# A fused attention and expert kernel: float32 score products for the third query group, half of the first group's scaling on ScalarE, and another order of the first loads

## The chip, the cores and the metric

The kernel runs on one core of one Trainium2 chip. The metric is the device time of one execution in microseconds, the median of the runs shown. A profiled execution has a time of its own, and next to it a span, from its first to its last instruction.

## What is computed

Windowed attention with a few sink keys feeds a dense two-layer block, and that feeds a router with eight experts:

```python
scores = q @ k.T / sqrt(64);  keep = (key < 4) | (0 <= query - key < 128)   # 2 batches, 8 heads, 768 tokens
a = softmax(where(keep, scores, -1e9));  x = heads_to_rows(a @ v)           # 1536 x 512
h = x @ w_in;  x = max(0.01 * h, h) @ w_out                                 # 512 -> 2048 -> 512
active = x @ w_skip > 0;  e = argmax(x @ w_gate);  g = softmax(x @ w_gate)[e]
out = x + active * g * (relu(x @ w1[e]) @ w2[e])                            # eight experts, 512 -> 1024 -> 512
```

All inputs are float32 (`w_in` and `w_out` come as 64-bit words that are decoded to float32 on the chip).

## The kernel before

The 1536 tokens are six **groups** of 256, numbered g = 0 to 5; so the "third group" is g = 2. Each group goes through attention (`attention`), then through 16 **chunks** f = 0 to 15 of the dense block (`chunk`): line 802 is a chunk's first product (12 matmuls of 256 columns into a tile `h`), line 823 its second (6 matmuls of 512 columns into `acc`, or into the tiles `S` and `PV` for g = 1). While group g's chunks run, group g+1's attention is to be done beside them. Only the chunks of g = 0 and g = 1 are interleaved with each other, since each decoded weight (`decode_w`, lines 704, 706, 708, 675 on VectorE and 668 on ScalarE) comes once and serves all groups. At the end come the experts (`plan_routed`).

Attention of a group has four head pairs p = 0 to 3 and, in each, two blocks of 128 queries qt = 0, 1. One (p, qt) is an **item** (`item`): scores for two heads, mask and row minimum on VectorE (552), exponential with row sum on ScalarE (555), the sum's reciprocal on VectorE (559, 560), scaling of the probabilities (567 on GpSimd, or 564 on ScalarE for g = 1), transposes (583, 605), the product with the values (622), and the copies that put the result where the dense block reads it (628 and 629, or 637, 638, 639 and then 668, 675).

There are two ways to be exact with float32 data:

- g = 0 and 1 (`self.whole`) form the scores as one float32 product (line 545). Queries are copied into a tile `qz` whose other 64 rows are zero, so one key tile serves both heads.
- g = 2 to 5 split queries and keys into a high and a low float32r half (`prep_split`, `queries`): the key tile is made twice, with two ScalarE copies (504) and two VectorE subtractions (506) for each p; the queries are transposed twice over (648), copied (650) and subtracted (651) for each item. Then the score is two products of one pass each (549). The sink keys have such halves too (`sink_keys`, 480 and 482); for g = 2 they are made early, from the first group's keys.

The order of the work on each engine is not written out by hand. `Plan.op` collects operations with an engine, a cost, tiles read and written, and a priority `pr`; `Plan.run` goes through them with those costs and, whenever an engine is free, takes the ready operation with the lowest `pr` whose tiles can be had. A tag such as `w`, `kT` or `T` has a fixed number of buffers, which are given out in the order in which the operations that first use them were written. So an operation can be ready and yet be passed over, because a tile written earlier in the code has not been taken. What comes out is one fixed list for each engine.

Loads of the first group are in `blocks`: keys on ScalarE's DMA queue, queries and values on SP's. `load_w` brings the dense weights (512 KB each) on SP's queue. `constants` builds masks on VectorE from two tiny loads, `lim`.

Of the kernel before, what the change touches and what calls it, by code (L numbers as in the profile page):

```python
# [39 lines left out]
def c_pool1(n):  # L40
    return 162 + 0.83 * n
# [184 lines left out]
class Arm:  # L226
# [4 lines left out]
    def __init__(self, tc, io, cst, scr, xg, window_attention):  # L231
        self.tc, self.nc, self.io, self.c, self.scr, self.xg = tc, tc.nc, io, cst, scr, xg
        self.fast = window_attention
        self.whole = (0, 1)
        self.B, self.H, self.S, self.D = io["q"].shape
# [69 lines left out]
    def attention(self, g):  # L305
# [23 lines left out]
    def blocks(self, g, b, qp):  # L329
# [5 lines left out]
        def ld(t, a, p0, p1):  # L335
# [3 lines left out]
            if t != "v":  # L339
                eng, dma = ("ACT", nc.scalar) if g == 0 and t == "k" else ("SP", nc.sync)  # L340
# [30 lines left out]
    def load(self, g, b, qp, p):  # L371
# [114 lines left out]
    def prep_split(self, g, qp, p):  # L486

        P, nc = self.p, self.nc
        pr = 16 * (g - 1) + 4 * p - 6.5
        rk, rv = self.rk, self.rv  # L490
# [17 lines left out]
        for h in range(2):  # L508
            P.op("POOL", c_pool1(32), lambda h=h: nc.gpsimd.tensor_scalar(
                out=kT[h].tile.rearrange("p (j c) -> p j c", c=144)[:, 0:2, 128:144], in0=self.kss[:, p, h:h + 1, :].bitcast(F32).to_broadcast([128, 2, 16]),  # L510
                scalar1=1.0, scalar2=1.0, op0=ALU.mult, op1=ALU.mult), r=[("kss", (p, h, i)) for i in range(2)], w=[(kT[h], "s")], pr=pr)

# [9 lines left out]
    def item(self, g, qp, p, qt, whole):  # L522
# [8 lines left out]
        if not whole:  # L531
            self.queries(g, p, qt, pr)
# [7 lines left out]
        for h in range(2):  # L540
            sp = P.buf(("S", "h", "h")[(4 * p + 2 * qt + h) % 3] if g == 0 else spare if g == 2 else "S", [128, 512])

            def score(sp=sp, h=h):
                if whole:
                    nc.tensor.matmul(out=sp.tile[:, 0:ncol], lhsT=self.qz.tile[:, p % 2, h, 128 * qt:128 * qt + 128], rhs=kT.tile[:, 0, c0:c0 + ncol], start=True, stop=True)
                    return
# [4 lines left out]
            P.op("PE", 4 * ncol / 2.4 if whole else 2 * c_mm(ncol), score, r=[(self.qz, (p % 2, h)), (self.qz, ("z", h)), kT] if whole else [*qT, kT[h]], w=[sp], pr=pr, hold=[A, nm, sm])  # L551
# [9 lines left out]
        for h in range(2):  # L561
            if g == 1:
# [713 lines left out]
def constants(nc, cp, pool, c, n_sink, window, E):  # L1276
# [5 lines left out]

    lim = T("lim", [128, 4], I32)
# [93 lines left out]
```

## Time and profile before

| | |
|---|---|
| median of 3 runs | 577.86 us (577.76 to 581.44) |
| profiled execution: its time | 577.76 us |
| profiled execution: its span | 576.0 us, so 1.76 us lie outside it |
| busy: TensorE 528.3, VectorE 412.3, ScalarE 345.3, GpSimd 172.8 us | 92%, 72%, 60%, 30% of the span |
| first scores | 10.87 us |
| first chunk of g = 2 goes on to its end from | 201.57 us |

A busy share is an average over parts with different limits: TensorE is idle or slow at the start, in one stretch near a third of the span, and at the end. Matmuls are pipelined, so that a busy TensorE is not one at its peak; what a matmul adds to a chain is read from the chain of waits, where an L802 of 12 matmuls takes 1.44 us.

### The profile page before, as it was taken

The numbers are of one execution on the slowest core, as the hardware profiler recorded it, in microseconds if no ns is written. First come the engines' busy times: TensorE is split into PE (matmuls) and PEld (weight loads), VectorE is DVE, ScalarE is ACT, GpSimd is POOL, SyncE is SP. The second block draws the span as 40 slices with busy tenths as digits, with TensorE's granted clock in tenths as the row PEclk, the third lists the DMA queues.
The fourth block names the chain that finished last, engine by engine and source line by source line (L and its number), as shares of the span: only waits on it lengthen the run. The fifth ranks groups of instructions, "written<-read, shape, count | busy, mean of one in ns | idle before, by whom it ended". The sixth has DMA issues, their size and how long they took to land.

```text
span 576.0 us, 10376 instructions
## 1 busy us (share of the span) xinstructions
PE 528.3 (92%) x3378; PEld 463.8 (81%) x3378; DVE 412.3 (72%) x1184; ACT 345.3 (60%) x892; POOL 172.8 (30%) x288
## 2 busy tenths in 40 slices
PE   3789999999999699999999999999999789999993
PEld 2668898878888588888899888999988678888772
DVE  3679999989678587668766786675746547767771
ACT  2669875554557466667656766555655356666760
POOL 3422201140143434333233333210221223443343
PEclk9989999999999699999999999999999889999997
DMA  6996543511112201222112230113465448888770
GB/s 148 281 317 235 193 141 119 146 50 52 56 44 60 53 21 37 49 53 73 40 36 51 47 83 15 25 48 137 138 194 171 161 156 286 265 273 287 250 261 21
DMA packets 81088, 72.99 MB, mean 127 GB/s; under 512 B 58579, under 2 KB 66771, under 8 KB 81024
## 3 DMA queue, kind: packets, MB, share of 16 engines
q1 hardware_dynamic: 77168, 70.67, 40.6%
q0 software_dynamic: 1600, 1.04, 0.6%
q10 hardware_dynamic: 2256, 0.53, 0.5%
q8 instruction: 29, 0.48, 0.4%
q14 instruction: 35, 0.29, 0.2%
HBM read 65.93 MB, written 10.51 MB: 133 GB/s over the span
## 4 chain that ended last, share of the span: by engine, by line
PE 64%; DVE 15%; ACT 7%; DMA 5%; POOL 4%; issue 4%; ACTq 0%; POOLq 0%; DVEq 0%
PE h L802 16%; PE acc L823 13%; PE acc L1043 5%; PE PV L622 4%; PE h L1027 3%; PE T L583 3%; DMA wm<-in_moe_w_dram 2%; POOL P L567 2%; PE S L1027 2%; PE S L549 2%; DVE C L638 2%; PE PV L1027 2%; PE T L897 2%; ACT P L555 2%; DVE P L552 2%
## 5 line engine op out<-in xcount | busy, mean ns | idle before, releaser
L802 PE MATMUL h<-x,w 128*128 128x256 f32 x1128 | 154.2, 286 | 3.0 <-DVE gl L816 1.8
L802 PEld LDWEIGHTS h<-x,w 128*128 128x128 f32 x1128 | 144.3, 190 | 8.1 <-DVE gl L816 3.2
L823 PE MATMUL acc<-w,gh 128*128 128x512 f32 x308 | 100.2, 406 | 0.0
L668 ACT ACTIVATE w<-wm 128x1024 fp32r<-128x1024 f32 x64 | 67.7, 1061 | 42.6 <-DMA wm<-in_moe_w_dram 26.6
L567 POOL TENSOR_SCALAR P<-P,s 128x272 f32<-128x272 f32 (+1 forms) x80 | 42.9, 550 | 114.7 <-DVE s L560 98.6
L675 DVE TENSOR_TENSOR w<-wm,w 128x1024 fp32r<-128x1024 f32 x48 | 60.2, 1262 | 17.3 <-ACT w L668 15.7
L675 POOL TENSOR_TENSOR w<-wm,w 128x1024 fp32r<-128x1024 f32 x16 | 38.8, 2427 | 93.3 <-ACT w L668 49.1
L555 ACT ACTIVATE P<-P,s 128x272 f32<-128x272 f32 (+1 forms) x96 | 50.0, 521 | 25.7 <-DVE s L552 25.2
L813 ACT ACTIVATE t<-h 128x256 f32<-128x256 f32 x94 | 35.8, 380 | 47.8 <-PE h L802 47.6
L823 PE MATMUL acc<-w,gl 128*128 128x512 f32 x156 | 61.3, 393 | 0.0
L823 PEld LDWEIGHTS acc<-w,gh 128*128 128x128 f32 x308 | 52.9, 189 | 7.2
L814 DVE TENSOR_TENSOR h<-h,t 128x256 f32<-128x256 f32 x94 | 40.2, 428 | 19.4 <-ACT t L813 18.6
L815 ACT ACTIVATE gh<-h 128x256 fp32r<-128x256 f32 x92 | 34.9, 379 | 19.1 <-DVE h L814 18.6
L816 DVE TENSOR_TENSOR gl<-h,gh 128x256 fp32r<-128x256 f32 x92 | 38.5, 418 | 10.9 <-ACT gh L815 9.9
L552 DVE CUSTOM_DVE_ANT_0 P<-S,mk 128x272 f32<-128x272 f32 (+1 forms) x70 | 28.9, 412 | 12.6 <-PE S L549 10.9
L823 PEld LDWEIGHTS acc<-w,gl 128*128 128x128 f32 x156 | 29.3, 188 | 6.8
L583 PE MATMUL T<-idt,P 128*128 128x128 f32 x152 | 27.7, 295 | 6.9 <-DVE kT L506 4.9
L583 PEld LDWEIGHTS T<-idt,P 128*128 128x128 f32 x152 | 22.7, 204 | 12.3 <-POOL P L567 4.5
L589 ACT ACTIVATE AT<-T 128x256 fp32r<-128x256 f32 x60 | 20.0, 383 | 13.5 <-PE T L583 12.7
L590 DVE TENSOR_TENSOR AT<-T,AT 128x256 fp32r<-128x256 f32 x60 | 23.4, 418 | 6.5 <-ACT AT L589 5.3
L638 DVE TENSOR_TENSOR C<-PV,C 64x256 f32<-64x256 f32 x48 | 20.3, 422 | 10.0 <-ACT C L637 6.5
L1043 PE MATMUL acc<-w,gT 128*128 128x512 f32 x96 | 24.5, 400 | 2.0 <-POOL w L675 1.6
(256 smaller groups left out, 1087.4 us busy)
## 6 DMA issues: line engine op xcount, KB each, us to landing
wm<-in_moe_w_dram SPq DMA_DIRECT2D x64, 512.0 KB, 4.7
w<-in_moe_w_in_dram SPq DMA_DIRECT2D x14, 512.0 KB, 5.7
w<-in_moe_w_out_dram SPq DMA_DIRECT2D x14, 512.0 KB, 6.8
rq<-in_q_dram SPq DMA_DIRECT2D x64, 64.0 KB, 2.1
out_dram<-x SPq DMA_DIRECT2D x12, 256.0 KB, 2.2
rk<-in_k_dram SPq DMA_DIRECT2D x24, 96.0 KB, 2.2
rv<-in_v_dram SPq DMA_DIRECT2D x24, 96.0 KB, 2.5
scr<-x SPq DMA_DIRECT2D x1, 2056.0 KB, 9.2
```

What stands on the lines that cost most here:

```text
L552: P.op("DVE", 66 + 1.07 * ncol, lambda sp=sp, h=h: nc.vector.tensor_tensor_reduce(out=A.tile[:, 0:ncol, h], in0=sp.tile[:, 0:ncol], in1=ma ...
L555: P.op("ACT", 280 + 0.83 * ncol, lambda h=h: nc.scalar.activation(out=A.tile[:, 0:ncol, h], in_=A.tile[:, 0:ncol, h], func=AF.Exp, scale=- ...
L567: P.op("POOL", 245 + 0.83 * ncol, lambda h=h: nc.gpsimd.tensor_scalar(out=A.tile[:, 0:ncol, h], in0=A.tile[:, 0:ncol, h], scalar1=sm.tile[ ...
L583: nc.tensor.transpose(tt.tile[:, 2 * j + h, :], A.tile[:, o:o + 128, h], c["idt"])
L668: nc.scalar.activation(out=at(0), in_=view(src.tile), func=AF.Copy)
L675: P.op(lo, {"DVE": c_dve(n), "POOL": c_pool2(n)}[lo], lambda: eng[lo].tensor_tensor(out=at(1), in0=view(src.tile), in1=at(0).bitcast(F32), ...
L802: nc.tensor.matmul(out=h.tile, lhsT=wi.tile[:, a, 128 * k:128 * k + 128], rhs=xT.tile[:, b, k, :], start=k == 0 and n == 0, stop=k == self ...
L814: P.op("DVE", c_dve(256), lambda: nc.vector.tensor_tensor(out=h.tile, in0=h.tile, in1=t.tile, op=ALU.max), r=[t], w=[h], pr=fast)
L816: P.op("DVE", c_dve(256), lambda: nc.vector.tensor_tensor(out=gl.tile, in0=h.tile, in1=gh.tile.bitcast(F32), op=ALU.subtract), r=[h, gh], ...
L823: nc.tensor.matmul(out=acc[i].tile, lhsT=a.tile[:, q], rhs=wo.tile[:, b, :], start=first and n == 0, stop=last and n == 2)
L1027: nc.tensor.matmul(out=hp[a].tile, lhsT=xt.tile[:, i, k, :], rhs=w1[k][j].tile[:, 512 * a:512 * a + 512], start=k == 0 and n == 0, stop=k ...
L1043: nc.tensor.matmul(out=yp.tile, lhsT=gt.tile[:, a, 2 * n + j, :], rhs=w2[n][b].tile[:, 512 * j:512 * j + 512], start=n == 0 and j == 0 and ...
```

## The change

There are three edits. `self.mixed = 2` gives g = 2 the float32 score products of the first two groups: `prep_mixed` makes one key tile and both blocks' queries for a head pair at once, and the queries are loaded once and not twice; the sink halves for g = 2 are not made any more. In `item`, the scaling of the second head of g = 0 goes from GpSimd to ScalarE. The third edit is in the first loads: `blocks` is called ahead of the zeroing of `qz`, the keys of p = 1 to 3 are issued on SP's queue, and a one-element exponential stands at the head of ScalarE's list.

```diff
@@ Arm.__init__
+        self.mixed = 2
@@ Arm.attention
         if whole:
+            self.blocks(g, b, qp)
             if g == 0:
                 self.qz = self.p.buf("w", [128, 2, 2, 256])
...
-            self.blocks(g, b, qp)
@@ blocks.ld
-                eng, dma = ("ACT", nc.scalar) if g == 0 and t == "k" else ("SP", nc.sync)
+                eng, dma = ("ACT", nc.scalar) if g == 0 and t == "k" and p0 == 0 else ("SP", nc.sync)
@@ load
-            two = 2 if t == "q" else 1
+            two = 2 if t == "q" and g != self.mixed else 1
@@ prep_split: its part on the keys is now prep_keys, without these lines
-        elif g - 1 in self.whole:
-            self.sink_keys(p, ("ks", p), lambda a: self.ks[a, p, :], pr)
@@ new
+    def prep_mixed(self, p, pr):
...
+        kT = self.kT = P.buf("kT", [128, 1, 432])
+        qT = self.qT = [P.buf("qT", [128, 256]) for _ in range(2)]
...
+        for h in range(2):
+            P.op("POOL", 100 + 0.9 * 256, lambda h=h: nc.gpsimd.memset(qT[h].tile[64 - 64 * h:128 - 64 * h, :], 0.0), w=[(qT[h], 0)], pr=pr - 1)
+        P.op("PE", 3 * C_TR, lambda: [nc.tensor.transpose(pk.tile[:, j, :], flat(rk, j), idt) for j in range(3)], r=[rk], w=[pk], pr=pr, hold=[kT])
...
+        P.op("ACT", c_act(384, True), lambda: nc.scalar.activation(out=col(0, 128), in_=pk.tile, func=AF.Copy), r=[pk], w=[(kT, 0)], pr=pr)
...
+        P.op("PE", 2 * C_TR, lambda: [nc.tensor.transpose(pq.tile[:, j, :], flat(rq, j), idt) for j in range(2)], r=[rq], w=[pq], pr=pr, hold=qT)
+        for h in range(2):
+            rows = slice(64 * h, 64 * h + 64)
+            P.op("ACT", c_act(256, True), lambda rows=rows, h=h: nc.scalar.activation(
+                out=qT[h].tile[rows, :], in_=pq.tile[rows].rearrange("p j c -> p (j c)"), func=AF.Copy, scale=-0.125), r=[pq], w=[(qT[h], 1)], pr=pr)
@@ prep_split
+        if g == self.mixed:
+            self.prep_mixed(p, pr)
+        else:
+            self.prep_keys(g, qp, p, pr)
@@ item
-        if not whole:
+        native = whole or g == self.mixed
+        if not native:
             self.queries(g, p, qt, pr)
...
-                if whole:
-                    nc.tensor.matmul(out=sp.tile[:, 0:ncol], lhsT=self.qz.tile[:, p % 2, h, 128 * qt:128 * qt + 128], rhs=kT.tile[:, 0, c0:c0 + ncol], start=True, stop=True)
+                if native:
+                    l = self.qz.tile[:, p % 2, h, 128 * qt:128 * qt + 128] if whole else qT[h].tile[:, 128 * qt:128 * qt + 128]
+                    nc.tensor.matmul(out=sp.tile[:, 0:ncol], lhsT=l, rhs=kT.tile[:, 0, c0:c0 + ncol], start=True, stop=True)
...
-            if g == 1:
+            if g == 1 or g == 0 and h:
@@ constants
+    warm = T("warm", [128, 1])
+    G.memset(warm, 0.0)
+    nc.scalar.activation(out=warm, in_=warm, func=AF.Exp)
     lim = T("lim", [128, 4], I32)
```

What this does to the lists of the engines is seen at three places. In these rows `w_...` are tiles of the tag `w` (weights, and raw keys, queries and values of the first groups), and a number behind a name tells the buffer. First SP's list from its first load, before:

```order
L1284 DMA lim<-in_n_sink_dram 128x2
L687 DMA wl_124<-in_moe_w_in_dram 128x4x256
L342 DMA w_128<-in_q_dram 128x2x64 x2
L342 DMA w_128<-in_q_dram 128x6x64 x2
L348 DMA w_133<-in_v_dram 128x4x64 x2
```

SP's list at the same place, with the change:

```order
L1320 DMA lim<-in_n_sink_dram 128x2
L343 DMA w_129<-in_q_dram 128x2x64 x2
L343 DMA w_125<-in_k_dram 128x6x64 x2
L343 DMA w_129<-in_q_dram 128x6x64 x2
L349 DMA w_131<-in_v_dram 128x4x64 x2
```

A 512 KB weight has left the head of the queue (it comes some 25 issues later), and the keys of p = 1 to 3 stand there, in front of the queries of p = 1 to 3.

Second, the head of ScalarE's list, before (`kT` keys, `ks` and `kss` sink keys, `P` probabilities):

```order
L1285 DMA lim<-in_window_dram 128x2
L342 DMA w_126<-in_k_dram 128x2x64 x2
L342 DMA w_126<-in_k_dram 128x6x64 x2
L453 ACT_TABLE_LOAD
L453 ACTIVATE kT_155<-T_154 128x2x128
L455 ACTIVATE ks<-T_154 128x16
L467 ACTIVATE w_122<-T_158 64x256
L480 ACTIVATE kss<-ks 64x16 x2
L555 ACTIVATE P_171,s_16_173<-P_171,s_15_172 128x128 x2
L555 ACTIVATE P_183,s_22_185<-P_183,s_21_184 128x272 x2
L453 ACTIVATE kT_204<-T_203 128x2x128
```

ScalarE's list at the same place, with the change:

```order
L1318 ACT_TABLE_LOAD
L1318 ACTIVATE warm<-warm 128x1
L1321 DMA lim<-in_window_dram 128x2
L343 DMA w_125<-in_k_dram 128x2x64 x2
L454 ACTIVATE kT_150<-T_149 128x2x128
L456 ACTIVATE ks<-T_149 128x16
L468 ACTIVATE w_139<-T_153 64x256
L588 ACTIVATE P_170,s_16_172<-P_170,s_15_171 128x128 x2
L588 ACTIVATE P_180,s_21_182<-P_180,s_20_181 128x272 x2
L597 ACTIVATE P_170<-P_170,s_16_172 128x128
L454 ACTIVATE kT_193<-T_192 128x2x128
```

The table load has come ahead of the two DMA issues, `kss` is gone, and the scaling of a second head (L597) stands between the exponentials and the next keys.

Third, TensorE at the hand-over from the chunks of g = 1 to those of g = 2, before; `acc_2608` is the product with the values of the last item of g = 2, `h_2463` the first chunk of g = 2, and L885, L897, `S_2616` and `S_2689` belong to the router of g = 1 and to the attention of g = 3:

```order
L622 MATMUL acc_2608<-sAT,vs_1226 128x256
L549 MATMUL S_2616<-kT_2531,qT_2536 128x128
L549 MATMUL S_2616<-kT_2531,qT_2537 128x128
L885 MATMUL T_2623<-idt,x_507_2293 128x128 x4
L648 MATMUL T_2633<-idt,rq_2467 128x128 x2
L897 MATMUL T_2655<-wl_2601,w_75 9x128 x12
L897 MATMUL T_2655<-wl_2624,w_75 9x128 x12
L549 MATMUL S_2689<-kT_2530,qT_2634 128x272
L549 MATMUL S_2689<-kT_2530,qT_2635 128x272
L802 MATMUL h_2463<-x_1890,w_365 128x256 x3
L802 MATMUL h_2705<-x_1890,w_462 128x256 x12
```

TensorE at the hand-over with the change; `acc_2477` is now the last item's product with the values, `h_2514` the first chunk of g = 2, and L856 the second products of the last two chunks of g = 1:

```order
L655 MATMUL acc_2477<-sAT,vs_1176 128x256
L681 MATMUL T_2487<-idt,rq_2260 128x128 x2
L856 MATMUL S_1359<-w_1818,gh_2438 128x512 x2
L856 MATMUL S_1359<-w_1818,gl_2445 128x512
L856 MATMUL PV_1360<-w_1818,gh_2438 128x512 x2
L856 MATMUL PV_1360<-w_1818,gl_2445 128x512
L835 MATMUL h_2514<-x_1908,w_365 128x256 x9
L856 MATMUL S_1359<-w_1892,gh_2502 128x512 x2
L856 MATMUL S_1359<-w_1892,gl_2506 128x512
L856 MATMUL PV_1360<-w_1892,gh_2502 128x512 x2
L856 MATMUL PV_1360<-w_1892,gl_2506 128x512
L835 MATMUL h_2514<-x_1908,w_365 128x256 x3
```

Before, the last second products of g = 1 are over by then: between them and the end of the first chunk of g = 2 stand the last two items of g = 2 with all their waits, and work for the router and for g = 3. With the change, two chunks' second products of g = 1 stand behind the last item, and the router's work and that of g = 3 come later, among the chunks of g = 2. Further on, the last item of g = 3 ends in the first chunk of g = 3, where it ended a chunk ahead of it before; from the fifth chunk of g = 5 on, TensorE's two lists are alike but for one place.

## Rows read from the trace of the kernel before

**Rows 1.** The page: TensorE's busy tenths and granted clock in 40 slices.

```profile
PE   3789999999999699999999999999999789999993
PEclk9989999999999699999999999999999889999997
```

**Rows 2.** Stretches: busy PE, PEld, DVE, ACT, POOL (instructions); granted clock; DMA share, GB/s.

```profile
20.00:40.00 20.00, 14.92 (x75) 12.02 (x74) 15.70 (x55) 11.92 (x42) 7.56 (x12) 0.83 1.13 278
40.00:60.00 20.00, 19.30 (x133) 16.94 (x132) 19.16 (x59) 18.37 (x55) 5.32 (x11) 1.00 0.73 251
...
180.00:200.00 20.00, 13.42 (x87) 11.93 (x86) 13.20 (x43) 11.33 (x37) 9.09 (x22) 0.78 0.25 68
```

**Rows 3.** The hand-over to g = 2 in stretches, the same columns.

```profile
184.40:191.15 6.75, 2.88 (x21) 2.29 (x20) 4.67 (x17) 4.03 (x15) 2.27 (x6) 1.00 0.41 124
191.15:201.40 10.25, 7.55 (x48) 6.99 (x47) 5.39 (x17) 4.59 (x14) 4.54 (x10) 0.50 0.18 41
```

**Rows 4.** Chain of waits: last values products and next chunk at both hand-overs (start, us).

```profile
193.96 1.28 PE acc L622 x6
...
201.57 1.79 PE h L802 x15
...
260.97 0.71 PE PV L622 x6
...
264.74 0.74 PE h L802 x4
```

**Rows 5.** Chain of waits: TensorE pieces, among them scores of either kind.

```profile
74.44 0.46 PE S L545 x2
...
143.47 0.25 PE T L549 x2
143.72 1.39 PE acc L823 x6
145.11 0.22 PE T L648 x2
```

**Rows 6.** Groups by line and shape (busy us, mean ns).

```profile
L651 DVE SCALAR_TENSOR_TENSOR qT<-T,qT 128x256 fp32r<-128x256 f32 x32 | 13.4, 419 | 0.6
L506 DVE TENSOR_TENSOR kT<-T,kT 64x384 fp32r<-64x384 f32 x24 | 13.3, 555 | 2.7 <-ACT kT L504 2.1
L564 ACT ACTIVATE P<-P,s 128x272 f32<-128x272 f32 x16 | 7.9, 547 | 0.3 <-DVE s L560 0.3
L482 DVE TENSOR_TENSOR kss<-ks,kss 64x16 fp32r<-64x16 f32 x8 | 1.7, 212 | 1.3 <-ACT kss L480 1.0
```

**Rows 7.** VectorE's L506 alone, then its L651, in stretches (busy us, count).

```profile
60.00:145.00 85.00, 2.22 (x4) 1.00 0.37 113
...
60.00:145.00 85.00, 1.24 (x3) 1.00 0.37 113
```

**Rows 8.** Chain of waits, first group: GpSimd's scaling.

```profile
26.02 0.89 POOL P L567 x2
...
27.07 2.38 POOL P L567 x2
...
36.45 1.06 POOL P L567 x2
...
37.71 1.35 POOL P L567
```

**Rows 9.** Timeline of the first 10 us (start, us).

```profile
1.24 0.42 SPq L687 DMA_DIRECT2D wl<-in_moe_w_in_dram  x1
...
6.88 1.28 ACT L453 ACT_TABLE_LOAD   x1 [6.88 <-DMA lim<-in_n_sink_dram]
...
8.75 0.30 DVE L1324 TENSOR_SCALAR mk<-mk 128x272 f32<-128x272 f32 x1
...
8.95 0.48 PE L449 MATMUL T<-idt,w 128*128 128x128 f32 x1 [0.39 <-DMA w<-in_k_dram]
...
9.89 0.43 DVE L464 TENSOR_SCALAR w<-T 64x256 f32<-64x256 f32 x1 [0.84 <-PE T L459]
```

More of the change, by code (lines that the diff above doesn't have):

```diff
@@ L484, in sink_keys, with prep_keys @@
                  r=[src, ("kss", (p, h, 0))], w=[("kss", (p, h, 1))], pr=pr)
[L486 to L490, printed above, removed]
+    def prep_keys(self, g, qp, p, pr):
+        P, nc, rk = self.p, self.nc, self.rk
         j0 = 1 if qp == 0 else 0
@@ L511, in prep_split @@
                 scalar1=1.0, scalar2=1.0, op0=ALU.mult, op1=ALU.mult), r=[("kss", (p, h, i)) for i in range(2)], w=[(kT[h], "s")], pr=pr)
+    def prep_mixed(self, p, pr):
+        P, nc, rk, rq, idt = self.p, self.nc, self.rk, self.rq, self.c["idt"]
+        kT = self.kT = P.buf("kT", [128, 1, 432])
+        qT = self.qT = [P.buf("qT", [128, 256]) for _ in range(2)]
+        pk = P.buf("T", [128, 3, 128])
+        pq = P.buf("T", [128, 2, 128])
+        flat = lambda x, j: x.tile[:, j, :, :].rearrange("p h d -> p (h d)")
+        for h in range(2):
+            P.op("POOL", 100 + 0.9 * 256, lambda h=h: nc.gpsimd.memset(qT[h].tile[64 - 64 * h:128 - 64 * h, :], 0.0), w=[(qT[h], 0)], pr=pr - 1)
+        P.op("PE", 3 * C_TR, lambda: [nc.tensor.transpose(pk.tile[:, j, :], flat(rk, j), idt) for j in range(3)], r=[rk], w=[pk], pr=pr, hold=[kT])
+        col = lambda a, n: kT.tile[:, 0, :].rearrange("p (j c) -> p j c", c=144)[:, :, a:a + n]
+        P.op("ACT", c_act(384, True), lambda: nc.scalar.activation(out=col(0, 128), in_=pk.tile, func=AF.Copy), r=[pk], w=[(kT, 0)], pr=pr)
+        P.op("POOL", c_pool1(32), lambda: nc.gpsimd.tensor_scalar(
+            out=col(128, 16)[:, 0:2], in0=self.ks[:, p:p + 1, :].to_broadcast([128, 2, 16]), scalar1=1.0, scalar2=1.0, op0=ALU.mult, op1=ALU.mult),
+            r=[("ks", p)], w=[(kT, "s")], pr=pr)
+        P.op("PE", 2 * C_TR, lambda: [nc.tensor.transpose(pq.tile[:, j, :], flat(rq, j), idt) for j in range(2)], r=[rq], w=[pq], pr=pr, hold=qT)
[3 more added lines that the diff above has]
+                out=qT[h].tile[rows, :], in_=pq.tile[rows].rearrange("p j c -> p (j c)"), func=AF.Copy, scale=-0.125), r=[pq], w=[(qT[h], 1)], pr=pr)
+    def prep_split(self, g, qp, p):
+        P, nc = self.p, self.nc
+        pr = 16 * (g - 1) + 4 * p - 6.5
+        rk, rv = self.rk, self.rv
+        j0 = 1 if qp == 0 else 0
+        nk = 3 - j0
+        if g == self.mixed:
+            self.prep_mixed(p, pr)
+        else:
+            self.prep_keys(g, qp, p, pr)
         vh = self.vh = P.buf("vhl", [128, 3, 2, 128], F32R)
@@ L549, in score @@
                     nc.tensor.matmul(out=sp.tile[:, 0:ncol], lhsT=qT[i].tile[:, h, :], rhs=kT[h].tile[:, c0:c0 + ncol], start=i == 0, stop=i == 1)
-            P.op("PE", 4 * ncol / 2.4 if whole else 2 * c_mm(ncol), score, r=[(self.qz, (p % 2, h)), (self.qz, ("z", h)), kT] if whole else [*qT, kT[h]], w=[sp], pr=pr, hold=[A, nm, sm])
+            P.op("PE", 4 * ncol / 2.4 if native else 2 * c_mm(ncol), score, r=[(self.qz, (p % 2, h)), (self.qz, ("z", h)), kT] if whole else [qT[h], kT] if native else [*qT, kT[h]], w=[sp], pr=pr, hold=[A, nm, sm])
             P.op("DVE", 66 + 1.07 * ncol, lambda sp=sp, h=h: nc.vector.tensor_tensor_reduce(
```

## The prediction

> **What bounds the kernel now.** I read the page's slices first [rows 1]: TensorE is near full from about 40 us to the end but for one slice that shows 6, and there its granted clock falls as well. The stretches say which engine ends last in each part [rows 2]. From 20 to 40 us no engine is full, so a chain of waits sets the pace: the first group's attention, with nothing to run beside it. From 40 us VectorE is busy 19.2 of 20, with TensorE at 19.3: the weights are decoded there, and VectorE is what a chunk waits for. From 180 to 200 us nothing is full again: TensorE 13.4, VectorE 13.2, clock 0.78. That is the hand-over from the chunks of g = 1, which are all done, to those of g = 2, which wait for the last two items of attention. In its two stretches [rows 3] TensorE is busy 2.88 of 6.75 us and 7.55 of 10.25; the second stretch has a granted clock of 0.50, which is 1.2 GHz where the rest has 2.4, after TensorE had stood idle for most of the first. So this hand-over loses 3.87 + 2.70 = 6.6 us idle, and half of 7.55 = 3.8 us by the clock, **10.3 us** together. That is the largest loss that the change can reach; the later groups have no such stretch.
>
> **The change part by part.** The sum is made against the profiled execution, 577.76 us (span 576.0 and 1.76 outside it), which lies 0.1 under the median of 577.86.
>
> First loads. Before, a 512 KB weight goes out on SP at 1.24 us, in front of the queries, and the first keys let TensorE start its second transposes at 8.95 [rows 9]. Taking the weight away saves at most its passage: at the 278 GB/s of the stretch from 20 to 40 us [rows 2], 1.9 us. Against it, ScalarE now loads its table, 1.28 us [rows 9], and runs one activation before it issues `lim` and the keys, so both start about 1.5 us later; the load was hidden before, in the wait for the keys. VectorE's masks cannot begin before `lim` lands and end at 9.05; the query copy of line 464, at 9.89, stands behind them on VectorE and would go to about 10.5. So this part lies between -1.9 and +1.5 us. I take **+0.4**, near the masks' delay, since keys that land early would wait for it. The Trainium skill ("ScalarE: Activation LUTs", What ACT_TABLE_LOAD costs) gives a load and its drain together 2.66 us; the trace's load of 1.28 agrees with the load alone, and no row here shows the drain, since ScalarE waited for the keys behind it. By the page's price the masks would slip 1.4 us more and the sum would end near 570.7.
>
> First group's scaling. Seven GpSimd scalings lie on the chain in four pieces of 0.89, 2.38, 1.06 and 1.35 us, 5.7 together [rows 8]. Half goes to ScalarE, so the pieces may halve: -2.8. ScalarE gets eight more activations, at most 0.547 each [rows 6] or 4.4 us, and loses the small `kss` copies. It was busy 11.9 of 20 there [rows 2], so it has room, but it works in order: the scaling waits for the reciprocal, and behind it queue the decode copies and the next exponentials. If that queue always bites, the gain is gone; bounds -2.8 and 0. I take **-2**.
>
> Decode part, 40 to 145 us. For g = 2 VectorE loses, for all four head pairs, eight subtractions on keys (0.555), eight on queries (0.419) and eight on sink keys (0.212) [rows 6], 9.5 us. Only four and three of the large ones fall before 145 us, 2.22 + 1.24 = 3.5 us [rows 7]; the small ones lie in the first 40 us, in the part that waits anyway. TensorE is almost as full in this part, so not all can show: bounds -3.5 and 0, and I take **-2**. ScalarE loses as well (one key copy in place of two); GpSimd gains eight small memsets and is busy 5.32 of 20 us [rows 2].
>
> Score products. One float32 product of 272 columns takes half of 0.92, or 0.46 us for a head with its two records; the split pair takes 0.25 [rows 5]. Sixteen products (four head pairs, two blocks, two heads) add 16 x 0.21 = 3.3 us. The queries need two transposes for a head pair in place of four, 0.11 each [rows 5]: eight fewer, -0.9. TensorE is at its bound, so **+2.4** is on the path; none of it is hidden. (The Trainium skill, "FP8 and Floating Point Precision", TensorE Precision Notes, counts four passes for true float32. Four passes at this trace's 0.125 would be 0.50, so the trace is a little under it; with 0.50 the sum would end at 569.9.)
>
> Hand-over to g = 2. In the new list the last product with the values stands ahead of two chunks' second products and of nine matmuls of the next chunk, and only the three behind those need the last head pair. The cover is 1.39 + 9 x 0.12 + 1.39 = 3.9 us [rows 5]. The chain to be covered took from 195.24 to 201.57 before, 6.3 us, partly at the low clock and with the router's work in between; at the next hand-over, at full clock, from 261.68 to 264.74, 3.1 us [rows 4]. So between 0 and 2.4 us are left open. I take 1.5, since some wait of the items before it will be left too: 10.3 - 1.5, or **-8.8**. The work that TensorE did inside the old stretch (half of it for the router of g = 1 and for g = 3) is not saved; it moves among the chunks of g = 2.
>
> Hand-over to g = 3. Its last item now ends behind the first nine matmuls of the chunk that needs it. Between them stand transposes and scores worth some 1.5 us, against a chain of 3.1 us at full clock or 6.3 as the worst row [rows 4]: cost 0 to 4.8. I take **+1.5**.
>
> Sum: 0.4 - 2 - 2 + 2.4 - 8.8 + 1.5 = -8.5, so **569.3 us**.
>
> **The rivals.** (1) *Deeper*: the second key tile. One key tile serves both heads, so the two buffers of the tag `kT` hold two head pairs of g = 2, and keys can be made a pair ahead. If the items then run far enough ahead, TensorE's small waits in 100 to 180 us go too, and both hand-overs are free: -2.8 - 3.5 - 10.3 + 2.4 = -14.2, or 563.5. For it speaks that VectorE has room behind the decoding, 13.2 of 20 us [rows 2]; against it, that TensorE's slices all show 9 there [rows 1].
>
> (2) *The wait moves on*: g = 3 begins its attention late, because its first two items were done in the old stretch. At the next hand-over the worst row's 4.8 us come in place of 1.5, and the first group gains nothing: 569.3 + 3.3 + 2 = 574.6. For it speaks the list, against it that the chain at full clock was 3.1.
>
> (3) *Slower*: TensorE pays and the stretch stays. If VectorE, not the items' own chain, holds the last two items back (it has the chunks' own copies and the router beside them), the chunks of g = 1 again run out first, and then the float32 products only add: +2.4, +1.5 for the late masks, +1.5 at g = 3, or 583.2. It decides when the last second product of g = 1 comes off TensorE before the last item's scores do. VectorE's 4.67 of 6.75 and 5.39 of 10.25 us there [rows 3] speak against it.
>
> (4) *The loads don't do what they say*: the keys land no sooner, because their issue slipped by 1.5 us. That is the upper bound of the first part, and alone makes 570.4.
>
> **How the numbers follow.** Forecast, with (4) inside it: 0.55, 566 to 572; deeper 0.17; the wait moves on 0.2; slower 0.08. A measurement of this kernel tells about 1%, 5.8 us, from no change. The range for 8 in 10 reaches into (1) and (2): 562 to 576; left out are (3) and the tails. Faster by over 1% means under 572.1: nearly all of the forecast and all of (1), 0.69. Within 1%: (2), the forecast's upper end and half of (3), 0.26. Slower by over 1%: 0.05.
>
> **What would show it.** Scores begin at 10.5 to 11.5 us (10.87 before). GpSimd's pieces on the chain before 40 us are half as long. No stretch near 185 us has a granted clock of 0.50, and the first chunk of g = 2 goes through before 188 us (201.57 before); the first of g = 3 starts 8 to 12 us sooner. From there the distance to before stays the same to the end. The prediction is wrong if the low clock is still there, if the decode part ends no sooner, or if the gain at g = 2 is lost again by g = 4.

## The result and the profile after

The changed kernel takes **564.84 us** (563.57 to 565.15), against 578.24 (577.76 to 581.44) of the kernel before: ratio **0.9753, 95% interval 0.9714 to 0.9791**. The forecast was 569.3, and 562 to 576 with its range. The profiled execution took 565.15, with a span of 563.3 (576.0 before).

The page's slices [rows 1]: the slice that showed 6, with its fallen clock, is gone; besides the last slice the clock now falls in one alone, which shows 6 in PEclk, some 13 us behind the last chunk, where the experts begin.

```profile
PE   4899999999999999989999999999999889999993
PEclk9999999999999999999999999999999699999997
```

Stretches of the changed kernel [rows 2, 3]; the last line is the hand-over from the last chunk of g = 1 to the first of g = 2.

```profile
20.00:40.00 20.00, 17.26 (x115) 14.24 (x113) 18.49 (x63) 18.56 (x59) 6.86 (x13) 1.00 0.97 296
40.00:60.00 20.00, 19.38 (x134) 17.44 (x134) 19.58 (x56) 16.74 (x49) 3.03 (x6) 1.00 0.89 316
180.00:200.00 20.00, 19.50 (x150) 17.86 (x150) 12.45 (x39) 11.58 (x35) 3.21 (x10) 1.00 0.19 54
174.50:179.90 5.40, 5.36 (x34) 4.68 (x33) 3.95 (x9) 2.93 (x7) 3.94 (x8) 1.00 0.00 0
```

From 20 to 40 us VectorE and ScalarE are now nearly full and the clock is whole. At the hand-over TensorE is busy 5.36 of 5.40 us. The chain there is TensorE's own queue [rows 4]: nine products of the new chunk, the six matmuls of one chunk's second product (`S` and `PV`), and the other three at once behind them, from where the chain goes on with the chunk after it.

```profile
177.41 1.08 PE h L835 x9
178.50 0.70 PE S L856 x3
179.20 0.68 PE PV L856 x3
179.88 1.79 PE h L835 x15
```

At the next hand-over, to g = 3, the timeline of TensorE shows what the prediction feared: nine products of the chunk, then 5.7 us until the other three, in which it has 3.86 us of other work.

```profile
240.19 1.22 PE L835 MATMUL h<-x,w 128*128 128x256 f32 x9
247.08 2.04 PE L835 MATMUL h<-x,w 128*128 128x256 f32 x15
```

Scores of g = 2 as two records of a float32 product (chain of waits), as long as the one of g = 1 in [rows 5]:

```profile
164.54 0.46 PE acc L578 x2
```

Groups by line and shape [rows 6]: 8 query subtractions (24 for 32) and 8 large key subtractions (16 for 24) fewer on VectorE; on ScalarE one scaling more for each item of g = 0, four of them of 272 columns (20 for 16).

```profile
L684 DVE SCALAR_TENSOR_TENSOR qT<-T,qT 128x256 fp32r<-128x256 f32 x24 | 10.1, 421 | 1.0 <-ACT qT L683 0.4
L503 DVE TENSOR_TENSOR kT<-T,kT 64x384 fp32r<-64x384 f32 x16 | 8.9, 555 | 2.1 <-ACT kT L501 1.5
L597 ACT ACTIVATE P<-P,s 128x272 f32<-128x272 f32 x20 | 10.1, 543 | 1.2 <-DVE s L593 1.1
```

The scaling on the chain of the first 40 us [rows 8]: one GpSimd piece is left of four, and three ScalarE pieces have come in:

```profile
13.15 0.30 ACT P L597
...
17.81 0.40 ACT P L597
...
25.87 1.28 POOL P L600
...
32.50 0.43 ACT P L597
```

The first 10 us [rows 9] (timeline: start, us):

```profile
0.78 1.28 ACT L1318 ACT_TABLE_LOAD   x1 [0.78 <-PEq L1395]
...
0.91 0.40 ACTq L1321 DMA_DIRECT2D lim<-in_window_dram  x1
...
1.34 0.97 ACTq L343 DMA_DIRECT2D w<-in_k_dram  x2
...
4.96 0.60 DVE L1323 CAST limf<-lim 128x4 f32<-128x4 int32 x1 [4.96 <-DMA lim<-in_window_dram]
...
7.68 0.30 DVE L1360 TENSOR_SCALAR mk<-mk 128x272 f32<-128x272 f32 x1
8.01 0.43 DVE L465 TENSOR_SCALAR w<-T 64x256 f32<-64x256 f32 x1
...
8.99 0.77 PE L578 MATMUL S<-kT,w 128*128 128x128 f32 x2 [2.19 <-ACT w L468]
```

ScalarE's requests leave while its table load runs; the masks end 1.07 us sooner than in [rows 9] and the first scores start at 8.99, not 10.87.

Where the time came from is best followed by the chunks. The table gives, for each traced execution, the start in us of a chunk's twelfth first product (line 802 before, 835 or near it after): the first chunk of g = 0, the last of g = 1, the first and last of g = 2, the first and last of g = 3, the first of g = 4 and its last, the last of g = 5. Chunks of g = 0 and g = 1 alternate; of these 32, the 24th is named at times below.

| kernel | g0 first | g1 last | g2 first | g2 last | g3 first | g3 last | g4 first | g4 last | g5 last | span |
|---|---|---|---|---|---|---|---|---|---|---|
| before | 48.1 | 178.1 | 201.6 | 260.4 | 265.2 | 329.4 | 334.1 | 395.4 | 442.0 | 576.0 |
| loads + scaling (e9) | 37.6 | 170.2 | 194.8 | 253.8 | 258.6 | 322.8 | 327.6 | 388.6 | 435.5 | 571.4 |
| products alone (e3) | 43.7 | 180.7 | 186.1 | 244.0 | 253.7 | 315.5 | 324.2 | 386.0 | 433.1 | 570.9 |
| changed | 37.7 | 174.5 | 179.9 | 237.8 | 247.4 | 309.2 | 317.9 | 379.4 | 426.5 | 563.3 |
| key tile held (e5) | 39.4 | 168.5 | 190.7 | 251.2 | 256.0 | 320.2 | 325.0 | 386.0 | 432.5 | 568.3 |
| and VectorE's work (e6) | 37.7 | 165.5 | 195.5 | 255.9 | 260.7 | 324.9 | 329.7 | 390.7 | 437.2 | 573.2 |
| g = 3 earlier (e8) | 37.8 | 174.8 | 179.8 | 239.6 | 246.5 | 313.5 | 318.2 | 379.2 | 426.6 | 561.4 |

### The profile page after: what moved, and what is told of

It reads as the page before. It is cut to its first block, busy times and chain, and to the rows that moved or that the text cites. A ratio compares the mean times of both kernels' runs of the same rounds, so it can differ in the third digit from the quotient of the medians.

```text
span 563.3 us, 10312 instructions
## 1 busy us (share of the span) xinstructions
PE 523.5 (93%) x3370; PEld 458.1 (81%) x3370; DVE 406.2 (72%) x1160; ACT 345.9 (61%) x889; POOL 170.0 (30%) x285
## 4 chain that ended last, share of the span: by engine, by line
PE 60%; DVE 12%; ACT 9%; DMA 8%; POOL 6%; issue 4%; POOLq 0%; SPq 0%; ACTq 0%; DVEq 0%
PE h L835 17%; PE acc L856 14%; DMA wm<-in_moe_w_dram 5%; PE acc L1076 3%; PE PV L655 3%; PE T L616 3%; POOL w L708 3%; ACT P L588 2%; PE h L1060 2%; PE S L582 2%; PE S L1060 2%; PE T L930 2%; DVE C L671 1%; PE PV L1060 1%; DVE P L585 1%
## 5 line engine op out<-in xcount | busy, mean ns | idle before, releaser
L856 PE MATMUL acc<-w,gh 128*128 128x512 f32 x308 | 100.1, 406 | 0.2 <-ACT gh L848 0.2
L708 DVE TENSOR_TENSOR w<-wm,w 128x1024 fp32r<-128x1024 f32 x48 | 61.9, 1302 | 20.6 <-ACT w L701 18.8
L600 POOL TENSOR_SCALAR P<-P,s 128x272 f32<-128x272 f32 (+1 forms) x72 | 36.5, 518 | 93.8 <-DVE s L593 74.9
L856 PE MATMUL acc<-w,gl 128*128 128x512 f32 x156 | 61.4, 394 | 0.0
L856 PEld LDWEIGHTS acc<-w,gh 128*128 128x128 f32 x308 | 53.3, 189 | 8.0 <-ACT gh L848 0.6
L849 DVE TENSOR_TENSOR gl<-h,gh 128x256 fp32r<-128x256 f32 x92 | 38.5, 419 | 10.2 <-ACT gh L848 9.5
L856 PEld LDWEIGHTS acc<-w,gl 128*128 128x128 f32 x156 | 29.3, 188 | 7.4 <-DVE gl L849 0.8
L672 POOL TENSOR_TENSOR xr<-C 128x128 f32<-128x128 f32 x32 | 15.6, 488 | 43.2 <-DVE C L671 43.0
L671 DVE TENSOR_TENSOR C<-PV,C 64x256 f32<-64x256 f32 x48 | 20.2, 422 | 11.2 <-ACT C L670 8.1
## 6 DMA issues: line engine op xcount, KB each, us to landing
out_dram<-x SPq DMA_DIRECT2D x12, 256.0 KB, 2.8
```

Source lines behind the costliest of these rows:

```text
L600: P.op("POOL", 245 + 0.83 * ncol, lambda h=h: nc.gpsimd.tensor_scalar(out=A.tile[:, 0:ncol, h], in0=A.tile[:, 0:ncol, h], scalar1=sm.tile[ ...
L708: P.op(lo, {"DVE": c_dve(n), "POOL": c_pool2(n)}[lo], lambda: eng[lo].tensor_tensor(out=at(1), in0=view(src.tile), in1=at(0).bitcast(F32), ...
L849: P.op("DVE", c_dve(256), lambda: nc.vector.tensor_tensor(out=gl.tile, in0=h.tile, in1=gh.tile.bitcast(F32), op=ALU.subtract), r=[h, gh], ...
L856: nc.tensor.matmul(out=acc[i].tile, lhsT=a.tile[:, q], rhs=wo.tile[:, b, :], start=first and n == 0, stop=last and n == 2)
```

## The experiments

Theory: each edit works by itself. The two at the start take the first group's losses away, and the float32 products close the hand-over to g = 2 because the items of g = 2 get shorter; a part of that is given back later. The rivals are that one edit carries all, that a key tile and not the work is the reason, and that the table load matters. The kernel before was timed again beside each, so effects are given as differences of ratios, times 578 us; each ratio is uncertain by some 0.003 to 0.006, or 2 to 3.5 us.

**e1, loads alone.** The other two edits are taken back:

```diff
-        self.mixed = 2
+        self.mixed = -1
@@ prep_keys
+        elif g - 1 in self.whole:
+            self.sink_keys(p, ("ks", p), lambda a: self.ks[a, p, :], pr)
@@ item
-            if g == 1 or g == 0 and h:
+            if g == 1:
```

> Only the edits at the start are left (the early table load, the first group's requests ahead of the weights', the rest of its keys on SP); VectorE scales as before and the third group has two-part scores. Theory A, from the changed kernel's trace (ScalarE's requests leave at 0.91 and 1.34 us, the first scores at 8.99 instead of 10.87): the start brings 1.9 us and no more, the low clock at 27 to 34 us stays, the whole takes 575 to 577 us. Theory B, that the earlier start brings most of the 9.6 us that the first group gained: the stretch of low clock near 27 us goes, the chain reaches 60 us some 8 us sooner, the whole takes 567 to 570.

577.3 us, ratio 0.9986 (0.9961 to 1.001): -0.8 us. Half of each theory held. The first chunk is reached at 37.0, 11.1 us sooner, and no low clock is left near 27 us (B); but at the first chunk of g = 2 only 5.2 us of it are left, and 2.8 at the last chunk of g = 5, and the time is near what A said.

**e2, scaling alone.** The products as in e1, and the loads taken back:

```diff
-        self.mixed = 2
+        self.mixed = -1
@@ attention
-            self.blocks(g, b, qp)
             if g == 0:
...
+            self.blocks(g, b, qp)
             xT = self.xt[g] = ...
@@ blocks
-... if g == 0 and t == "k" and p0 == 0 else ("SP", nc.sync)
+... if g == 0 and t == "k" else ("SP", nc.sync)
@@ constants
-    warm = T("warm", [128, 1])
-    G.memset(warm, 0.0)
-    nc.scalar.activation(out=warm, in_=warm, func=AF.Exp)
```

> Only the scaling of every second head of the first group on ScalarE is left. Theory A: it brings the larger part of the 9.6 us that the first group gained (some 7.7 without the loads), since no chunk waits for VectorE's scaling any more and TensorE does not fall to the low clock at 27 to 34 us; if the later stages pass it on, 568 to 571 us. Theory B: it brings the 2 us of the prediction, 575 to 576.5. In both the hand-over to the third group keeps its low clock near 190 us.

573.76 us, ratio 0.9909 (0.9883 to 0.9935): -5.3 us. The time lies between the two ranges; the trace is that of theory A. The first chunk comes at 38.4, 9.7 us sooner, with no low clock near 27 us either, and from the hand-over on the distance to the kernel before stays at 5.9 to 6.3 us as far as the last chunk. The two edits of the start do not add up in the first chunk (37.0, 38.4, and 37.6 for both): either one takes the same loss away. At the end they do, as -0.8 and -5.3 against -5.9 (e9).

**e3, products alone.** The loads taken back as in e2 and the scaling as in e1.

> Only the float32 score products of the third group are left. Theory A: the hand-over to the third group gains 10 to 13 us by itself, of which some 5 to 9 are given back by 440 us; 567 to 572 us, with the first chunk of the third group 10 us or more sooner and nothing changed ahead of 140 us. Theory B, that the hand-over only opens because the first group is ahead: the low clock near 190 us stays and the whole takes 574 to 579.

570.36 us, ratio 0.9847 (0.979 to 0.9905): -8.8 us. Theory A: the first chunk of g = 2 comes 15.5 us sooner, the last of g = 5 still 8.9. The first chunk of g = 0 came 4.4 us sooner as well, where of this edit only the small sink halves are missing; the 24th chunk came only 1.0 sooner.

**e4, without the loads.** Only the loads taken back, as in e2.

> The changed kernel without its edits at the start: scaling and score products are left. Theory A (parts add): 1.9 us slower than the changed kernel, 566 to 567.5 us. Theory B (what comes early is waited for later, so that the end does not see it): within 0.5 us of the changed kernel's 564.8. Theory C (the start carries the first group): 571 or more.

566.83 us, ratio 0.9817 (0.9758 to 0.9876), 3.7 us above the changed kernel by the ratios and 2.0 by the medians; the spans are equal (563.5 and 563.3). The equal spans are no sign for B: the last chunk of g = 5 comes 3.4 us later (429.9 against 426.5), and what lies behind it, which no edit touches, was 3.2 us shorter in this one execution. By the times A and B can't be told apart at this size; C is out.

**e5, key tile held.** Each head pair of g = 2 takes both buffers of `kT`, as it did before:

```diff
@@ prep_mixed
+        self.k2 = P.buf("kT", [128, 432])
...
-             r=[rk], w=[pk], pr=pr, hold=[kT])
+             r=[rk], w=[pk], pr=pr, hold=[kT, self.k2])
@@ item, scores
-             hold=[A, nm, sm])
+             hold=[A, nm, sm, self.k2] if g == self.mixed else [A, nm, sm])
```

> The changed kernel, but every head pair of the third group also holds the second key tile until its scores are done, as the two-part products did; no instruction is added. Theory A (shorter steps give the gain at the hand-over; a query tile is held by each head pair anyway): within 1.5 us of the changed kernel, 564 to 566.5 us, and the hand-over to the third group stays without a gap. Theory B (the first rival of the prediction, a second key tile that lets the next head pair's preparation start early): half of the gap or more comes back, 5 us or more, 570 to 574 us.

569.64 us, ratio 0.9827 (0.9778 to 0.9875): 4.3 us lost. Between the theories: from the last chunk of g = 1 to the first of g = 2 there are 22.2 us again (5.4 in the changed kernel), 16.8 more. But the last chunk of g = 1 comes 6.0 sooner, since less of the attention stands ahead of it, so the first chunk of g = 2 is 10.8 later, and 4.3 reach the end.

**e6, VectorE's work put back.** As e5, with four instructions for each head pair into the held tile:

```diff
@@ prep_mixed
+        for h in range(2):
+            a, z = slice(64 * h, 64 * h + 64), slice(64 - 64 * h, 128 - 64 * h)
+            P.op("DVE", c_dve(384), lambda a=a, z=z: nc.vector.tensor_tensor(
+                out=k2.tile[z, :].rearrange("p (j c) -> p j c", c=144)[:, :, 0:128], in0=pk.tile[a, :, :], in1=col(0, 128)[a], op=ALU.subtract),
+                r=[pk, (kT, 0)], w=[(k2, h)], pr=pr)
...
+        for h in range(2):
+            P.op("DVE", c_dve(256), lambda: nc.vector.tensor_scalar(
+                out=k2.tile[:, 0:256], in0=pq.tile.rearrange("p j c -> p (j c)"), scalar1=-0.125, scalar2=None, op0=ALU.mult), r=[pq], w=[k2], pr=pr)
```

> As the run before it, with VectorE's work put back too: for each head pair of the third group the two subtractions of key halves (0.42 us each) and two instructions on the queries (0.39 us), all into the held tile, which nothing reads; 6.5 us of VectorE in all. Theory A1 (VectorE's load sets the hand-over): 4 to 6.5 us of the gap come back, 569 to 572 us. Theory A2 (the chain from transposes to scores is shorter by a subtraction, and VectorE has room): less than 1.5 us beyond the run before it.

575.25 us, ratio 0.9934 (0.9905 to 0.9963): another 6.2 us lost. The instructions put back take more than the expectation said, 4.4 and 3.4 us (groups by line and shape, e6), 7.8 in all, and no engine reads what they write. Theory A1 in kind; the time is 3.3 us above its range, which stood on a run with the held tile that would lose nothing.

```profile
L527 DVE TENSOR_TENSOR kT<-T,kT 64x384 f32<-64x384 f32 x8 | 4.4, 555 | 0.8 <-ACT kT L523 0.7
L535 DVE TENSOR_SCALAR kT<-T 128x256 f32<-128x256 f32 x8 | 3.4, 422 | 1.2 <-PE T L533 1.1
```

The stretch from 180 to 200 us, of e5 and then of e6:

```profile
180.00:200.00 20.00, 16.84 (x120) 14.72 (x121) 13.61 (x44) 12.17 (x37) 7.07 (x16) 0.91 0.15 36
```

```profile
180.00:200.00 20.00, 14.73 (x81) 12.99 (x82) 9.69 (x29) 9.13 (x27) 5.69 (x12) 0.57 0.10 23
```

VectorE is busy 13.61 and 9.69 of 20 us, so it is not full in either. What fits is that its instructions stand in the items' way, one behind the other; TensorE runs dry and its granted clock falls, to a mean of 0.57 in e6. But the planner made another list too: the 24th chunk comes at 128.3 (135.1 in e5), with 603 matmuls from the first chunk to it (631 in e5), so more of the other work was left behind it. What the work costs and what the other list costs were not told apart.

**e7, no early table load.** The three lines of `warm` go.

```diff
@@ constants
-    warm = T("warm", [128, 1])
-    G.memset(warm, 0.0)
-    nc.scalar.activation(out=warm, in_=warm, func=AF.Exp)
```

> The changed kernel without the early table load. Theory A (from the changed kernel's trace: ScalarE's requests leave at 0.91 and 1.34 us although the load runs from 0.78 to 2.06): the requests leave at the same times, the first scores come within 0.3 us of 8.99, and the table load of 1.28 us stands ahead of ScalarE's first copy, near 6.5 us; 564.5 to 566.5 us. Theory B (the prediction's: the load holds ScalarE's requests by up to 1.5 us): without it the requests leave 0.5 us or more sooner and the first scores come before 8.2.

564.64 us, ratio 0.9754 (0.9703 to 0.9805): the same. ScalarE's first instructions then (timeline):

```profile
0.78 0.41 ACTq L1318 DMA_DIRECT2D lim<-in_window_dram  x1
1.22 1.00 ACTq L343 DMA_DIRECT2D w<-in_k_dram  x2
2.25 1.28 ACT L454 ACT_TABLE_LOAD   x1 [2.25 <-issue]
```

The requests leave 0.13 and 0.12 us sooner, not 1.5: theory A for the requests. Against A, the table load does not stand ahead of the first copy: it runs at 2.25, in the wait for the keys. It had stood late in the kernel before [rows 9] because four key requests came first (timeline, before); with two of them on SP it is hidden without any help. The chunks come at the same times within 0.5 us.

```profile
1.23 5.62 ACTq L342 DMA_DIRECT2D w<-in_k_dram  x4
```

**e8, g = 3 earlier.** Against the loss after 240 us:

```diff
@@ order
-        ... - (21 if g < 2 else 10 if g == 2 else 5)
+        ... - (21 if g < 2 else 10 if g == 2 else 8 if g == 3 else 5)
```

> The changed kernel with the fourth group's attention (g = 3) three ranks earlier in the planner, 8 instead of 5. Theory A (what is lost between 240 and 425 us, some 7 us, is lost since the attention of g = 3 and after starts relative to the chunks some 5 to 8 us later than before the change): TensorE's idle time from 238 to 379 us falls by 2 us or more, 561 to 563.5 us. Theory B (these losses come from something that the order doesn't move, such as the length of an item): 564 to 567 us, the loss only moves.

562.8 us (562.4 to 563.11), ratio 0.9715 (0.9674 to 0.9755). Theory A by its time and by the idle time of TensorE: from the last chunk of g = 2 to that of g = 4 there are, of before, of e9, of the changed kernel and of e8:

```profile
260.50:395.50 135.00, 132.44 (x950) 120.62 (x950) 95.15 (x331) 83.09 (x252) 39.98 (x88) 1.00 0.19 50
```

```profile
253.80:388.60 134.80, 132.49 (x950) 120.68 (x949) 95.32 (x331) 83.40 (x253) 40.06 (x88) 1.00 0.19 51
```

```profile
237.80:379.40 141.60, 135.30 (x965) 122.37 (x965) 99.83 (x347) 87.16 (x266) 44.29 (x96) 1.00 0.17 43
```

```profile
239.60:379.20 139.60, 136.37 (x971) 123.56 (x971) 99.62 (x347) 87.04 (x265) 43.81 (x96) 1.00 0.19 46
```

With the gap at g = 2 the stretch lasts 134.8 to 135.0 us (e2, e5 and e6 too: 134.8), without it 141.6 to 142.0 (e3: 142.0). Of the 6.6 us more, 2.9 are TensorE's work (15 instructions more) and 3.7 its idle time (6.30 for 2.56); e8 takes the idle time to 3.23. Yet its chunks end no sooner, 426.6 against 426.5 at the last of g = 5: what the stretch gains, the chunks of g = 2 had lost (59.8 us from first to last, 57.9 in the changed kernel). In these two traces the 1.9 us of the spans lie behind the chunks, where the low clock lasted 10.2 us in the changed kernel and 3.4 in e8 and no edit is. So where e8's 2 us come from is not shown.

**e9, no products.** The changed kernel with `self.mixed = -1` and the branch of e1.

> The changed kernel without its float32 score products: loads and scaling alone. Theory A (the three edits add up, as 0.7 + 4.2 + 7.6 us against 13.4 for all): 572.5 to 574 us, with the gap at the hand-over to the third group near 190 us as before; the run with the held tile and VectorE's work put back (575.25) is then 1 to 2.5 us above it, which is what the products cost TensorE. Theory B (the edits overlap): below 570 us, or above 576.

572.07 us, ratio 0.9898 (0.9868 to 0.9928): -5.9 us for the two edits of the start. Theory A in its main part: -5.9 and -8.8 make -14.7, and the changed kernel has -14.3. The median is 0.4 us under the range given. e6 lies 2.1 us above it by the ratios, give or take 2.4: what is left of the products once tile and work are put back.

**e10, g = 3 to 5 earlier.** As e8, for all later groups:

```diff
-        ... 10 if g == 2 else 5)
+        ... 10 if g == 2 else 7)
```

> The changed kernel with rank 7 instead of 5 for all groups from the fourth on. Theory A (the later groups' attention starts too late against the chunks): what the run with the fourth group alone gained (2.0 us) and up to 2 us more from the fifth and sixth: 560.5 to 562.8 us, with less idle TensorE after 379 us too. Theory B (only the fourth group was late, since its slack was the gap that the change removed): the same as that run within 1 us, or slower, since earlier items press on the chunks of the group before.

563.43 us, ratio 0.9759 (0.9698 to 0.982). Theory B by its time; nothing more is gained.

**e11, g = 3 scaled half on ScalarE.** As e8, and:

```diff
-            if g == 1 or g == 0 and h:
+            if g == 1 or g in (0, 3) and h:
```

> The run with the fourth group's attention three ranks earlier, and every second head of that group scaled on ScalarE instead of GpSimd. Theory A (the length of one item of the fourth group, with its 1.0 us on GpSimd in the chain, sets the loss that is left from 206 to 313 us, 10.9 us of idle TensorE): 560 to 562 us. Theory B (the loss that is left is queues on VectorE and ScalarE, and more work on ScalarE lengthens them): 562.8 to 565 us.

564.84 us, ratio 0.9774 (0.9712 to 0.9836). Its time fits B, but it doesn't test it: with ScalarE's new costs the planner made another list, and the stretch of e8's table is back at 141.9 us (240.7 to 382.6).

**e12, e8 without the early table load.** The diffs of e7 and e8 together.

> The run with the fourth group's attention three ranks earlier, without the early table load. Theory A (the load ahead brings nothing, as its own run showed, and the earlier rank brings 2 us): 562 to 563.5 us, a ratio of 0.970 to 0.9735. Theory B (the 2 us of the earlier rank were a draw of the runs): 564 to 565.5 us, the ratio of the changed kernel, 0.9755 to 0.978.

562.76 us (561.7 to 562.9), ratio 0.9731 (0.9703 to 0.9759). Theory A. e8 and e12 lie 2 us under the changed kernel and e7 (564.84, 564.64) in their medians; the intervals of the ratios overlap, so the 2 us are likely and not certain. e8 and e12 are the fastest versions that the runs gave; they can't be told apart.

## Why the prediction was right, and where it was off

The sign, the range and the largest part held. The measured 564.84 lies 4.5 us under the forecast, below the forecast's own 566 to 572, and nearer to rival 1's 563.5 than to 569.3. The sum said -8.5 us and the ratios give -14.3: 5.8 short, 4.3 of it in the first group and 1.5 in the four terms of the products. Its terms, with what the runs gave:

| term | forecast | measured |
|---|---|---|
| first loads | +0.4 | -0.8 alone (e1) |
| first group's scaling | -2 | -5.3 alone (e2); both -5.9 (e9) |
| decode part | -2 | -2.1 by the 24th chunk (changed against e9) |
| score products | +2.4 | +2.1, give or take 2.4 (e6 against e9) |
| hand-over to g = 2 | -8.8 | -12.8 from the 24th chunk to the first of g = 2, with the products' own cost in it (changed against e9) |
| hand-over to g = 3, and later | +1.5 | +5.9 by the last chunk of g = 5 |

**First group.** The two terms said -1.6 and the runs -5.9: this is the step that was mis-sized. Two things were read too small. The prediction let the four GpSimd pieces halve, -2.8 at most; on the chain of the changed kernel one piece of 1.28 us is left of 5.7, and ScalarE's 0.30, 0.40 and 0.43 have come in, 3.3 less. And it did not price the clock of 0.83 that stands in [rows 2]. In the kernel before TensorE ran at the low level there:

```profile
27.30:34.10 6.80, 6.25 (x24) 5.30 (x25) 4.16 (x10) 2.30 (x6) 2.22 (x3) 0.50 1.08 363
```

The same eight products with the values took twice as long on the chain as before it fell (chain of waits, before):

```profile
20.88 0.89 PE PV L622 x8
...
30.90 1.71 PE PV L622 x8
```

TensorE had been idle for more than half of the time ahead of that stretch (busy 1.93 of 4.50 us):

```profile
22.80:27.30 4.50, 1.93 (x11) 1.36 (x12) 3.97 (x17) 3.36 (x14) 1.49 (x4) 1.00 1.35 220
```

Either early edit alone was enough for a full clock from 26 to 36 us; with the products alone it was low for 3.4 us. So the prediction priced the loss at g = 2 with its clock and the same kind of loss here without; priced alike, half of the 6.25 us of busy time would be another 3.1, an estimate. The two sizes together, 6.4, fit the 5.9, but the clock's part was not shown by itself. For e1 took the low clock away too, was 11.1 us ahead at the first chunk, and kept 0.8: it lost 3.7 of its lead at the hand-over to g = 2 and 2.3 among the chunks of g = 3, where e9 lost 1.1 and 0.1. Why was not tried.

**First loads.** The assumption that the table load holds back ScalarE's requests was wrong (0.91 and 1.34 us, with the load from 0.78 to 2.06), and so rival 4, which rested on it, did not happen. `lim` landed 1.8 us sooner, the masks followed, and the first scores gained 1.9, where the prediction had them between 10.5 and 11.5. The Trainium skill ("ScalarE: Activation LUTs", What ACT_TABLE_LOAD costs) gives 2.66 us for load and drain; here the load took 1.28, the activation behind it began at 2.07 and the time was the same with this early load and without it (e7), so the page's price was not paid.

**Decode part.** This term came out as forecast. In e9 the first chunk comes at the same time (37.6, and 37.7 in the changed kernel), and the 24th of the 32 chunks of g = 0 and g = 1 comes at 136.8, against 134.7. From the first chunk to the 24th, e9 and then the changed kernel:

```profile
37.60:136.80 99.20, 95.05 (x637) 85.12 (x636) 96.01 (x251) 66.50 (x183) 19.64 (x32) 1.00 0.47 150
```

```profile
37.70:134.70 97.00, 95.28 (x634) 85.75 (x633) 93.94 (x240) 65.55 (x179) 19.27 (x32) 1.00 0.47 154
```

VectorE is busy 97% of both, and the stretch is shorter by what VectorE lost, 2.2 and 2.1 us. Between e2 and e4, which have no loads, it is 1.5. Against the kernel before this can't be seen, since there the start differs by 10.4 us.

**Score products.** 0.46 us a head, as in [rows 5], and 2.1 us at the end against 2.4, though the 2.1 is not clear of the noise. (The four passes of the Trainium skill, "FP8 and Floating Point Precision", TensorE Precision Notes, would have been 0.50 by the trace's 0.125; the trace has the 0.46.)

**Hand-over to g = 2.** The mechanism held in the lists: one chunk's second product, nine products, another second product, three more, no wait. Measured against e9 the first chunk of g = 2 came 14.9 us sooner, 12.8 of it behind the 24th chunk. The stretch from the last chunk of g = 1 to the first of g = 2 fell by 19.2 us (24.6 to 5.4), more than the whole loss of 10.3, since TensorE's work inside it left it too: 114 matmuls in e9, 34 now. The prediction said that this work is not saved, and moves among the chunks of g = 2. It went to two places. Ahead of the last chunk of g = 1, where the prediction had no term, more items of g = 2 cost 6.4 us from the 24th chunk on (e9, then the changed kernel):

```profile
136.80:170.20 33.40, 32.90 (x235) 29.39 (x234) 25.21 (x87) 19.37 (x57) 10.07 (x19) 1.00 0.14 38
```

```profile
134.70:174.50 39.80, 37.88 (x261) 33.27 (x260) 26.48 (x104) 24.80 (x79) 14.53 (x32) 1.00 0.15 39
```

And the router's 32 matmuls did move among the chunks of g = 2, but these take no longer, 57.9 us for 59.0: part of the attention of g = 3 has left them in exchange. Between the first and the last chunk of g = 2 stand the transposes of g = 3's probabilities, all 28 in e9 and 20 in the changed kernel, whose other 8 come behind the last chunk, and in the changed kernel the router's products (groups by line in that stretch, e9 and then the changed kernel):

```profile
L618 PE MATMUL T<-idt,P 128*128 128x128 f32 x28 | 5.7, 306 | 1.3 <-POOL P L602 0.7 <-DVE kT L505 0.6
```

```profile
L616 PE MATMUL T<-idt,P 128*128 128x128 f32 x20 | 4.1, 303 | 0.9 <-DVE kT L503 0.9
...
L930 PE MATMUL T<-wl,w 128*9 128x128 f32 x24 | 1.9, 229 | 0.0
```

So g = 3 is late, and that is the other step that failed: *from there the distance stays the same to the end*. Against e9 the distance goes from 14.9 us at the first chunk of g = 2 to 16.0 at its last, 11.2 at the first of g = 3 (9.6 us from the last chunk, 4.8 in e9: the upper bound of that term), 13.6 at its last, 9.7 at the first of g = 4, and 9.0 at the last of g = 5. The next two hand-overs, to g = 3 and g = 4, take 4.8 and 3.9 us more than in e9. e8, which begins g = 3 sooner, shortens the first of them to 6.9 us and the second to 4.7, and pays for it among the chunks; a run with the gap held open by nothing else was not made. Rival 2 named this with its reason and its 4.8 us, for g = 3 alone; its other half, that the first group gains nothing, did not come. Net, the products' four terms said -6.9 us and gave -8.4 by the ratios (9.0 by the last chunk of g = 5): the hand-over's gain and the later loss were both larger than said, by 6.4 and 4.4 us, and that they partly cancel is luck.

**Rival 1** was half of the mechanism, without its other gains: the waits of TensorE ahead of g = 2 did not go, and the hand-over to g = 3 was not free, so that its 563.5 is near the measured time is luck. Holding the second key tile costs 4.3 us (e5, give or take 3.5) and VectorE's work 6.2 more (e6), each with the list that the planner made for it. The 2.1 of e6 against e9 is the rest that makes up the 8.4 between e9 and the changed kernel, and no check of the other two. Which of the removed VectorE instructions counts, those on keys or those on queries, was not tried apart; nor was a second pair of key tiles with two-part products.

**Rival 3** is out: no gap at g = 2 in any kernel with the products unless work or tile were put back.

**Left open.** At the end of the chunks the clock falls for 6.8 us before (457.4 to 464.2) and 10.2 after (439.6 to 449.8), and for 3.4 to 10.2 in the other runs, though no edit touches that place. It is part of why the span gains 12.7 us where the last chunk of g = 5 gains 15.5. What lies behind the chunks took from 133.6 us (e4) to 138.7 (e1) in the traces.

## What to carry to other kernels

Price a chain of waits together with the clock of its stretch: a wait that lets TensorE's clock fall costs its own length, and the work behind it takes twice as long while the clock is low (0.89 and 1.71 us here), at the first stage as at the worst one. Then ask what of it the end will see: 11.1 us at the first chunk were 0.8 at the end in e1. A gap at one hand-over is also time in which the next stages' preparation gets ahead, so ask where the work inside it will go, and follow a closed gap through the next two hand-overs before counting it; here 19.2 us of it were 14.9 at the next chunk and 8.4 at the end. And take the removed work and the freed buffer as two prices: runs that put back one and then both tell them apart, as far as the planner's list stays the same.

## What the runs showed of the hardware

A table load on ScalarE runs beside the requests that ScalarE issues: load from 0.78 to 2.06 us, requests at 0.91 and 1.34. The start of a run differs from one execution to the next. The engines' lists are the same in the changed kernel and in e11 as far as about 169 us, by the tiles and shapes of their instructions, and from 15 to 18 us the one got through 24 matmuls and the other through 14, busy all the time (stretches, changed and then e11):

```profile
15.00:18.00 3.00, 3.00 (x24) 2.67 (x24) 1.97 (x11) 2.68 (x12) 1.14 (x5) 1.00 1.09 358
```

```profile
15.00:18.00 3.00, 3.00 (x14) 2.88 (x14) 0.89 (x5) 1.74 (x7) 0.96 (x4) 1.00 1.11 362
```

The first chunk came 1.7 us later in e11, and so it did in e5 (39.4). So one trace carries some 2 us of the start that no edit made, which is as much as e4, e8 and e11 differ by; the medians and ratios are what such differences can be judged on.
